# S4 convolution beside multi-query attention on Trainium2: the query projection in m-tiles of 128 rows, with heads that lie across two tiles

## The chip, the cores and the metric

The kernel runs on one core of one Trainium2 chip. The metric is the device time of one execution in microseconds; before the change its median is 1229.37 us over three runs. The core has five engines that matter here: TensorE (PE; its weight loads are listed apart as PEld), VectorE (DVE), ScalarE (ACT), GpSimd (POOL) and SyncE (SP). SP, ACT and POOL also issue DMAs, each in the order of its own instructions. TensorE writes only to PSUM, from where VectorE or ScalarE take the result.

## The reference: what is computed

Two independent parts, joined on the last axis. Part A convolves an input of 2048 steps and 576 channels with a kernel made from 128 complex modes per channel (an S4 layer). Part B is attention with 32 query heads of 18 columns that share one key and one value head:

```python
q = (x @ wq).reshape(B, S, 32, 18).transpose(0, 2, 1, 3)   # x: 1 x 2048 x 576
k = x @ wk
v = x @ wv
scores = einsum("bhqd,bkd->bhqk", q, k) * 18 ** -0.5
o = einsum("bhqk,bkd->bhqd", softmax(scores), v)
b = o.transpose(0, 2, 1, 3).reshape(B, S, 576) @ wo
```

Everything is float32.

## The kernel before

The program is one stream of instructions per engine, for TensorE, ScalarE and VectorE in an order that Python writes out while it builds the kernel.

**Attention** goes through four chunks of 512 queries. Within a chunk it goes through eight groups of four heads, and within a group through 16 blocks of 128 keys; two heads at a time form a pair. For each pair and key block, `scores` (L412, matmuls at L419) makes keys times queries in PSUM with a two-pass float32r product, 55 rows deep: 18 rows of the rounded query against the rounded key, 18 against the key's remainder, 18 of the query's remainder against the rounded key, and a row that holds a bound to be subtracted. `exponentials` (L427) applies exp on ScalarE, and `product` (L711, L718) multiplies with the values, four heads side by side in four column tiles of 32 of the array. Three pairs form one round of the main loop (L730); `step` counts key blocks of four heads, 512 in all.

**The query projection** fills gaps of this loop. `qproj` (L313) makes one m-tile, up to 126 of the 576 query rows (seven heads, the last m-tile has 72 rows and four heads, `MT` at L28) for the 512 queries of a chunk. It goes over two column halves of 256 and five k-slices of 128; each of these ten units is a `matmul4` (L164), which puts up to four column tiles of 32 rows into the array, one matmul each. In the trace each float32 matmul is two instructions. VectorE copies the result out of PSUM as `qh` (rounded), makes the remainder `ql` and the row maximum `ab` (L331 to L334). `qh` and `ql` have one buffer each. `queries` (L350) stores `qh` twice and `ql` once into the DRAM tensor `qd` of the chunk (L368, on POOL's queue; for chunk 0's first tile on SP's), so that each head finds its rows for the augmented product. Then it makes `aw`, the row maxima times the largest key of each row (`kmax`), sums them by head with a small matmul against the selector `sel` (`up`, L379), takes the maximum over heads on VectorE (`un`), and stores the negative as the bound's row (`sh`, L390 to L399). `fetch` (L402) brings a pair's rows back from `qd` into one of five `aug` buffers, on SP's queue, as soon as the whole pair has been stored and a buffer is free.

**The order of the fill work.** `fill` (L680) decides between rounds what else TensorE does: `prep` (normalizing), `side` (projections and output projection) and `conv` (part A). A planner's clock (class `Clock`, L61) carries estimated times; a unit of the query projection is charged 0.465. `late` (L633) compares the units done with a target at each quarter of the loop; the comparison at L694 holds `side` back when it is ahead of 0.64 units a step. Part A's sine batches on ScalarE wait until eight units of side work are due beside them, or 16 steps have passed (L1257 to L1261).

**The opening** (`setup`, L209). Inputs are loaded on the SP and ACT queues. TensorE projects the keys and chunk 0's first m-tile together, k-slice by k-slice (L268 to L270). `place(c)` (L278) puts the keys of chunk c into the augmented key tensor `kaug` with six DMAs on SP. The order on SP is: keys of chunk 0, of chunk 1, the stores of chunk 0's first m-tile, keys of chunks 2 and 3, then the weights of m-tiles 2, 3 and 4 (L295 to L300). Weights 0 and 1 are loaded earlier. The main loop starts with key chunk 0 and reaches chunk 2 at its ninth key block.

The program keeps a second, general attention behind a flag that is only taken when the bound is large (L784); with these inputs it does not run.

Of the kernel before, what the change touches and what calls it, by code (L numbers as in the profile page):

```python
# [17 lines left out]
P = 128  # L18
# [8 lines left out]
DT = KT[:4] + [(512, 64)]  # L27
MT = [(0, 126), (126, 126), (252, 126), (378, 126), (504, 72)]  # L28
# [143 lines left out]
class Attention:  # L172
# [33 lines left out]
    def load_wq(self, m):  # L206
        self.nc.sync.dma_start(self.wq[m], self.a["wq"][m, :, :, :MT[m][1]])

    def setup(self, tp, conv):  # L209
# [6 lines left out]
        self.wq = [cp.tile([P, 5, n], F32, name=f"wq{m}_sb") for m, (_, n) in enumerate(MT)]  # L216
        self.wo = cp.tile([P, 5, D], F32, name="wo_sb")
        self.sel = cp.tile([P, 8], F32, name="sel_sb")
        spread = tp.tile([P, 130], F32, name="spread_sb")
# [3 lines left out]
        self.kmax = cp.tile([P, 1], F32, name="kmax")  # L223
# [17 lines left out]
        nc.scalar.dma_start(self.wq[0], a["wq"][0, :, :, :MT[0][1]])  # L241
# [5 lines left out]
        nc.scalar.dma_start(self.sel, a["sel"][:, 0:8])  # L247
        nc.scalar.dma_start(spread, a["sel"][:, 8:138])
# [26 lines left out]
        V.tensor_scalar(km[:, 0:4], spread[:, 126:130], km[:, 4:5], None, op0=ALU.mult)  # L275
# [8 lines left out]
        nc.tensor.matmul(pk[:126, :], spread[:, 0:126], km[:, 0:4], start=True, stop=True)  # L284
# [5 lines left out]
        V.tensor_reduce(self.kmax[:126, :], pk[:126, :], axis=AX.X, op=ALU.max)  # L290
# [22 lines left out]
    def qproj(self, c, m, xt):  # L313

        nc, V, K = self.nc, self.V, self.k
        m0, mn = MT[m]
        self.q_left = 10
        yield "p", K.fill, False
        ps = self.bank(CT, f"q{c}_{m}")
        for f in range(2):  # L320
            sl = slice(f * 256, f * 256 + 256)
            for k in range(5):
                matmul4(nc, ps[:, sl], self.wq[m][:, k, :], xt[:, k, sl], start=(k == 0), stop=(k == 4))
                K.pe(0.465)
                self.q_left -= 1
                self.units += 1
                if (f, k) != (1, 4):
                    yield "p", 0.0, True
        K.v = max(K.v, K.t)
        qh, ql, ab = self.operands(c, m)  # L330
        V.tensor_copy(qh[:mn, :], ps[:mn, :])  # L331
        V.tensor_tensor(ql[:mn, :], ps[:mn, :], qh[:mn, :].bitcast(F32), op=ALU.subtract)
        K.filled()
        V.tensor_reduce(ab[:mn, 0:1], qh[:mn, :].bitcast(F32), axis=AX.X, op=ALU.max, apply_absolute_value=True)  # L334
        yield from self.queries(c, m, qh, ql, ab)

# [5 lines left out]
    def first_queries(self, ps):  # L342
        nc, V, mn = self.nc, self.V, MT[0][1]
        qh, ql, ab = self.operands(0, 0)
        nc.scalar.activation(qh[:mn, :], ps[:mn, :], AF.Copy)
        V.tensor_reduce(ab[:mn, 0:1], ps[:mn, :], axis=AX.X, op=ALU.max, apply_absolute_value=True)
        V.tensor_tensor(ql[:mn, :], ps[:mn, :], qh[:mn, :].bitcast(F32), op=ALU.subtract)
        yield from self.queries(0, 0, qh, ql, ab)

    def queries(self, c, m, qh, ql, ab):  # L350

        nc, V, K = self.nc, self.V, self.k
        m0, mn = MT[m]
        h0, h1 = m0 // DH, (m0 + mn) // DH
        if m == 0:
            self.qd[c] = self.dr.tile([H, 55, CT], F32, tag="qd", name=f"qd{c}")
        qd = self.qd[c]

        n0 = 4 if (c, m) == (0, 0) else 0
        for h in range(n0):  # L360
            t = self.aug[h // 2]
            for row, src in ((0, qh), (18, qh), (36, ql)):
                b = 64 * (h % 2) + row
                q = nc.scalar if h // 2 == 1 and row < 36 else nc.gpsimd
                q.dma_start(t[b:b + 18, :].bitcast(F32), src[h * DH:h * DH + DH, :].bitcast(F32))
        def store(q):
            for row, src in ((0, qh), (18, qh), (36, ql)):
                q.dma_start(qd[h0 + n0:h1, row:row + 18, :], src[n0 * DH:mn, :].bitcast(F32))  # L368
        if n0 == 0:
            store(nc.gpsimd)  # L370
        self.first = False
        yield "v", 0.0, False
        aw = self.p2.tile([P, P], F32, tag="aw", name=f"aw{c}_{m}", bufs=1)

        V.tensor_scalar(aw[:mn, :], ab[:mn, 0:1].broadcast_to([mn, P]), self.kmax[:mn, 0:1], 1.002, op0=ALU.mult, op1=ALU.mult)
        yield "p", max(K.v + 0.4, K.fill), False

        up = self.bank(8, f"up{c}_{m}")
        matmul4(nc, up, aw[:mn, :], self.sel[:mn, 0:8])  # L379
        K.pe(0.1)  # L380
        K.v = max(K.v, K.t + 0.3)
        un = self.p2.tile([P, 1], F32, tag="un", name=f"un{c}_{m}", bufs=4)
        V.tensor_reduce(un, up, axis=AX.X, op=ALU.max)
        K.filled()
        if self.ubound is not None:
            u2 = self.p2.tile([P, 1], F32, tag="u2", name=f"u2_{c}_{m}", bufs=4)
            V.tensor_tensor(u2, un, self.ubound, op=ALU.max)
            un = u2
        self.ubound = un
        sh = self.p2.tile([8, CT], F32R, tag="sh", name=f"sh{c}_{m}", bufs=1)  # L390
        V.tensor_scalar(sh, un[0:8, 0:1].broadcast_to([8, CT]), -1.0, None, op0=ALU.mult)
        for pr in range(n0 // 2):
            (nc.scalar, nc.sync)[pr].dma_start(self.aug[pr][54:119:64, :].bitcast(F32), sh[0:2, :].bitcast(F32))
# [5 lines left out]
        q.dma_start(qd[h0 + n0:h1, 54, :], sh[:h1 - h0 - n0, :].bitcast(F32))  # L399
        self.queried = c * H + h1  # L400
# [204 lines left out]
    def prepare(self):  # L605

        nc = self.nc
        while True:
            if not self.todo:
                yield "w", 0.0, False  # L610
                continue
            c, ms = self.todo[0]

            while ms[0] == 0 and (self.outs or c == NCH - 1 and self.due < 1 << 30):
                yield "w", 0.0, False
            self.todo.pop(0)
            self.busy = True
            if c == NCH - 1 and ms[0] == 0:
                self.part = self.xp.tile([P, 4, D], F32, tag="x", name="part")
                self.rest = {(t, n, m) for t in range(4) for n in range(2) for m in range(4)}  # L620
            if ms[0] == 3:
                self.w4 = self.p1.tile([P, D], F32, tag="ob", name="w4")
                self.b4 = self.p2.tile([P, P], F32, tag="aw", name="b4", bufs=1)
                nc.sync.dma_start(self.w4, self.a["wo4"])
                nc.sync.dma_start(self.b4, self.a["b4"])
            yield from self.normalize(c, ms)
            if c < NCH - 1:
                self.begin_output(self.outproj(c))
            elif ms[0] < 3:
                self.begin_output(self.outproj_part(c, ms, self.part))  # L630
            self.busy = False

    def late(self):  # L633

        s = self.step
        if self.due < 128 and self.due - s < 2 * self.q_left + 14:
            return True
        return (90, 180, 270, 302)[s // 128] - self.units > LEFT * (128 * (s // 128) + (120, 120, 120, 116)[s // 128] - s)
# [18 lines left out]
    def main(self, conv, flag):  # L657
# [22 lines left out]
        def fill(then):  # L680
# [3 lines left out]
            while more:  # L684
# [4 lines left out]
                for st in (prep, side, conv) if urgent else (prep, conv, side):  # L689
# [4 lines left out]
                    wait = then - K.t - (1.2 if st is side and not urgent and not side.holds and self.units > 0.64 * self.step + HEAD else 0.15)  # L694
# [89 lines left out]
def general_attention(tc, a, flag):  # L784
# [3 lines left out]
    with ExitStack() as ctx:  # L788
# [3 lines left out]
        wq = cp.tile([P, 5, 5, 126], F32, name="gwq")  # L792
# [12 lines left out]
        nc.sync.dma_start(wq, a["wq"].rearrange("m p k n -> p m k n"))  # L805
# [15 lines left out]
        with tc.For_i(0, 16, 1) as i:  # L821
# [4 lines left out]
            for h in range(H):  # L826
                ps = ps_t.tile([P, CT], F32, tag="t", name=f"gq{h}")
                for k, (k0, kn) in enumerate(KT):
                    nc.tensor.matmul(ps[:DH, :P], wq[:kn, h // 7, k, h % 7 * DH:(h % 7 + 1) * DH], xt[:kn, k, :], start=(k == 0), stop=(k == 4))
# [473 lines left out]
def layout(inputs):  # L1303
# [6 lines left out]
    wq = np.zeros((640, 630), np.float32)  # L1310
    wq[:D, :D] = g["B_wq"]
    a["wq"] = np.ascontiguousarray(wq.reshape(5, P, 5, 126).transpose(2, 1, 0, 3))
# [11 lines left out]
    sel = np.zeros((P, 138), np.float32)  # L1324
    i = np.arange(126)
    sel[i, i // DH] = 1.0
    for c in range(NCH):
        sel[32 * c + i % DH, 8 + i] = 1.0
        sel[32 * c:32 * c + 32, 134 + c] = 1.0
# [41 lines left out]
```

## Time and profile before

| | |
|---|---|
| runs | 1229.19, 1229.37, 1229.40 us |
| the profiled execution's own time | 1229.19 us |
| its span in the profile | 1226.8 us |
| TensorE clock granted, mean | 0.991 |
| HBM traffic | 55.64 MB read, 42.89 MB written |
| products with the values on TensorE (L718) | 518.0 us busy, 4096 instructions |
| scores on TensorE (L419) | 361.2 us busy, 2048 instructions |

The profile shows one execution, with times from the start of its span. A group's row reads: line, engine, operation, what it writes and reads with the shapes, how many; then busy microseconds, mean nanoseconds of one; then the idle time of the engine just before them and what ended it. Busy time of a group on TensorE is the union of instructions that overlap in the array, so the mean of one is no price. A row of the timeline reads: start, duration of the merged stretch, engine, line, operation, count, and in brackets the idle time before. The chain that ended last goes back from the end, at each step to what released it. A line can be a helper's: L99, L103, L107 and L111 are the recording wrappers around VectorE's operations, L169 is `matmul4`.

### The profile page before, as it was taken

The numbers are of one execution on the slowest core, as the hardware profiler recorded it, in microseconds if no ns is written. First come the engines' busy times: TensorE is split into PE (matmuls) and PEld (weight loads), VectorE is DVE, ScalarE is ACT, GpSimd is POOL, SyncE is SP. The second block draws the span as 40 slices with busy tenths as digits, with TensorE's granted clock in tenths as the row PEclk, the third lists the DMA queues.
The fourth block names the chain that finished last, engine by engine and source line by source line (L and its number), as shares of the span: only waits on it lengthen the run. The fifth ranks groups of instructions, "written<-read, shape, count | busy, mean of one in ns | idle before, by whom it ended". The sixth has DMA issues, their size and how long they took to land.

```text
span 1226.8 us, 32559 instructions
## 1 busy us (share of the span) xinstructions
PE 1145.4 (93%) x13762; PEld 471.2 (38%) x13762; DVE 991.1 (81%) x1604; ACT 1032.7 (84%) x1091; POOL 53.8 (4%) x93
## 2 busy tenths in 40 slices
PE   5799999999889999989999989999989999899997
PEld 1343334434333434434434433444333444334333
DVE  4667988987986995897895997796899897797753
ACT  2588998879978887898988998888989988999992
POOL 2010100000100000000000000000010000000000
PEclk9899999999999999999999999999999999999999
DMA  7542223122233112033123121312222312012111
GB/s 221 170 117 83 85 105 117 38 76 92 85 131 114 45 61 85 30 119 95 65 90 110 63 88 38 102 55 91 67 80 103 114 36 82 17 48 86 44 41 41
DMA packets 57947, 102.07 MB, mean 83 GB/s; under 512 B 14524, under 2 KB 25148, under 8 KB 57285
## 3 DMA queue, kind: packets, MB, share of 16 engines
q1 hardware_dynamic: 47029, 85.31, 21.0%
q0 software_dynamic: 10080, 14.05, 4.3%
q8 instruction: 110, 1.80, 0.6%
q10 hardware_dynamic: 688, 0.57, 0.2%
q14 instruction: 40, 0.33, 0.1%
HBM read 55.64 MB, written 42.89 MB: 80 GB/s over the span
## 4 chain that ended last, share of the span: by engine, by line
PE 62%; DVE 22%; ACT 7%; issue 5%; DMA 3%; SPq 1%; ACTq 0%; DVEq 0%
PE ops L718 25%; PE s L419 18%; ACT P L427 7%; DVE acc L99 4%; PE op L169 4%; DVE ks L99 3%; PE q L169 3%; PE kg L1081 3%; PE iy L169 3%; DVE tab L99 3%; DVE pt L99 2%; DMA xr<-xT 2%; PE hu L169 1%; PE lu L169 1%; PE hk L169 1%
## 5 line engine op out<-in xcount | busy, mean ns | idle before, releaser
L427 ACT ACTIVATE P<-s 128x1024 f32<-128x1024 f32 x1024 | 967.8, 1030 | 156.7 <-PE s L419 151.9
L718 PE MATMUL ops<-P,v_sb 128*32 128x512 f32 x4096 | 518.0, 599 | 7.3 <-DVE o L103 7.2
L419 PE MATMUL s<-aug,kaug 55*128 55x512 f32 x2048 | 361.2, 441 | 23.6 <-ACT P L427 19.9
L419 PEld LDWEIGHTS s<-aug,kaug 55*128 55x128 f32 x2048 | 168.8, 185 | 332.1 <-ACT P L427 298.0
L718 PEld LDWEIGHTS ops<-P,v_sb 128*32 128x32 f32 x4096 | 116.9, 110 | 151.4 <-issue 115.7
L169 PE MATMUL q<-x,wq_sb 128*32 128x256 f32 (+2 forms) x1480 | 105.4, 402 | 6.2 <-DMA wq_sb<-wq 4.6
L169 PE MATMUL op<-wo_sb,oT 126*32 126x288 f32 (+1 forms) x1088 | 78.3, 410 | 8.9 <-DVE ob L103 7.2
L169 PEld LDWEIGHTS q<-x,wq_sb 128*32 128x32 f32 (+1 forms) x1480 | 46.8, 111 | 61.6 <-issue 33.4
L103 DVE COPY ksb<-kg 128x192 f32<-128x192 f32 x48 | 17.4, 362 | 55.2 <-PE kg L1081 55.0
L99 DVE TENSOR_TENSOR tab<-tab,tt 128x576 f32<-128x576 f32 (+1 forms) x72 | 59.2, 822 | 1.8
L99 DVE TENSOR_TENSOR tab<-tab 128x576 f32<-128x576 f32 (+1 forms) x72 | 59.1, 822 | 1.7
L99 DVE TENSOR_TENSOR tt<-f,sum 128x576 f32<-128x576 f32 (+1 forms) x72 | 58.9, 818 | 0.0
L99 DVE TENSOR_TENSOR tab<-sum,r 128x576 f32<-128x576 f32 (+1 forms) x72 | 58.9, 818 | 0.0
L99 DVE TENSOR_TENSOR tab<-r,dif 128x576 f32<-128x576 f32 (+1 forms) x72 | 58.8, 817 | 0.0
L169 PEld LDWEIGHTS op<-wo_sb,oT 126*32 126x32 f32 (+1 forms) x1088 | 30.9, 109 | 50.2 <-issue 19.4
L99 DVE TENSOR_TENSOR acc<-acc,pt 128x1728 f32<-128x1728 f32 (+2 forms) x36 | 48.7, 1354 | 0.7
L99 DVE TENSOR_TENSOR pt<-us,ks 128x1728 f32<-128x1728 f32 (+2 forms) x36 | 48.7, 1352 | 0.4
L368 POOL DMA_DIRECT2D qd<-qh x38 | 24.0, 637 | 505.0 <-DVE qh L103 505.0
L169 PE MATMUL iy<-w,dft_sb 128*32 128x192 f32 x768 | 38.3, 335 | 7.6 <-DVE ql L99 7.4
L1081 PEld LDWEIGHTS kg<-tab 128*32 128x32 f32 x2304 | 35.8, 110 | 25.1 <-issue 7.3
L1081 PE MATMUL kg<-tab 128*32 128x64 f32 x2304 | 41.8, 220 | 1.8 <-DVE ql L99 1.2
L99 DVE TENSOR_TENSOR ks<-ks 128x576 f32<-128x576 f32 (+1 forms) x48 | 40.9, 853 | 0.7
(130 smaller groups left out, 916.1 us busy)
## 6 DMA issues: line engine op xcount, KB each, us to landing
aug<-qd SPq DMA_DIRECT2D x124, 110.0 KB
od<-o SPq DMA_DIRECT2D x31, 256.0 KB
qd<-qh POOLq DMA_DIRECT2D x30, 252.0 KB, 5.3
fr<-stage SPq DMA_DIRECT2D x10, 624.0 KB
u<-u SPq DMA_DIRECT2D x12, 384.0 KB
kd<-ksb SPq DMA_DIRECT2D x12, 384.0 KB
kt<-kd SPq DMA_DIRECT2D x48, 96.0 KB
outa<-u SPq DMA_DIRECT2D x12, 384.0 KB
```

The costliest lines, as they stand in the source:

```text
L99: return self.v.tensor_tensor(out, *a, **k)
L103: return self.v.tensor_copy(out, *a, **k)
L169: nc.tensor.matmul(ps[j:e], w[:, j:e], x, start=start, stop=stop, tile_position=(0, j))
L368: q.dma_start(qd[h0 + n0:h1, row:row + 18, :], src[n0 * DH:mn, :].bitcast(F32))
L419: nc.tensor.matmul(ps[:, j, :], self.kaug[r, kb * P:(kb + 1) * P], t[r, :], start=True, stop=True)
L427: nc.scalar.activation(pt, ps, AF.Exp, scale=SCALE)
L718: nc.tensor.matmul(o_ps[32 * j:32 * j + 32, :], self.v[:, kb, :], pts[2 * n + j // 2][:, j % 2, :], start=(kb == 0), stop=(kb == 15), tile ...
L1081: nc.tensor.matmul(ps[32 * g:32 * g + 32, d, :], t[:, :32], t[:, 32:], start=(j == 0), stop=(j == 1), tile_position=(0, 32 * g))
```

## The change

The m-tiles become 128, 128, 128, 128 and 64 rows, so that a head of 18 rows can begin in one tile and end in the next. Heads are counted to the tile in which they end (7, 14, 21, 28, 32, as before).

- `qproj`: the first four m-tiles keep two column halves of five k-slices, with four column tiles of 32 rows. The last one, 64 rows, takes both column halves at once: column tiles 0 and 1 hold its rows for queries 0 to 255, tiles 2 and 3 for queries 256 to 511. It has five units, and `qh`, `ql`, `ab` work on 256 columns.
- `pieces` and `store`: the rows of a tile go to `qd` in pieces, an end of a head, a run of whole heads, a beginning of a head; the last tile's in two column halves as well.
- `up`: for m-tiles 1 to 4 a second product adds the previous tile's share of the head that lies across (`self.aw` is the previous `aw`, which therefore has two buffers).
- `kmax` has a column for each m-tile; four of them come from new small products (`kmx4`) in the opening.
- `sh` is 256 columns wide and is read twice by its DMA.
- The opening's order on SP: weights of m-tile 2, keys of chunk 2, weights of 3, keys of chunk 3, weights of 4.
- The planner's targets follow the new number of units (80, 165, 250, 282 instead of 90, 180, 270, 302; 0.60 instead of 0.64 units a step). The general attention and the host's layout follow the new weights' shape.

```diff
+MQ = [(0, 128), (128, 128), (256, 128), (384, 128), (512, 64)]
+HQ = (0, 7, 14, 21, 28, 32)
...
         side.advance()
-        for c in range(2, NCH):
-            place(c)
 
         for m in range(2, 5):
             V.memset(self.wq[m][0:1, 0, 0:1], 0.0)
             self.load_wq(m)
+            if m < 4:
+                place(m)
         project(pv, 32, 4)
         V.tensor_copy(vt, pv)
+
+        pk = self.bank(16, "kmx4")
+        for m in range(1, 5):
+            for b, n in ((0, 128),) if m < 4 else ((0, 64), (64, 64)):
+                nc.tensor.matmul(pk[b:b + n, 4 * m - 4:4 * m], spread[:, 2 * m:2 * m + n], km[:, 0:4], start=True, stop=True, tile_position=(0, b))
+        V.tensor_reduce(self.kmax[:, 1:5], pk.rearrange("p (m c) -> p m c", c=4), axis=AX.X, op=ALU.max)
...
-        for f in range(2):
-            sl = slice(f * 256, f * 256 + 256)
+        for f in range(nf):
             for k in range(5):
-                matmul4(nc, ps[:, sl], self.wq[m][:, k, :], xt[:, k, sl], start=(k == 0), stop=(k == 4))
+                for j in range(4):
+
+                    o = slice(32 * j, 32 * j + 32)
+                    i = o if m < 4 else slice(32 * (j % 2), 32 * (j % 2) + 32)
+                    x = slice(256 * f, 256 * f + 256) if m < 4 else slice(256 * (j // 2), 256 * (j // 2) + 256)
+                    nc.tensor.matmul(ps[o, 256 * f:256 * f + 256], w[:, k, i], xt[:, k, x], start=(k == 0), stop=(k == 4), tile_position=(0, 32 * j))
...
+    @staticmethod
+    def pieces(m, h0):
+
+        m0, mn = MQ[m]
+        i = max(m0, h0 * DH)
+        while i < m0 + mn:
+            h, d = divmod(i, DH)
+            n = (m0 + mn - i) // DH if d == 0 else 0
+            rows = (n, 0, DH) if n else (1, d, min(DH - d, m0 + mn - i))
+            yield (i - m0, h) + rows
+            i += rows[0] * rows[2]
...
         def store(q):
             for row, src in ((0, qh), (18, qh), (36, ql)):
-                q.dma_start(qd[h0 + n0:h1, row:row + 18, :], src[n0 * DH:mn, :].bitcast(F32))
+                for i, h, n, d, nd in self.pieces(m, n0):
+                    for f in range(1 if m < 4 else 2):
+                        cs, i1 = (slice(0, CT), i) if m < 4 else (slice(256 * f, 256 * f + 256), i + 64 * f)
+                        q.dma_start(qd[h:h + n, row + d:row + d + nd, cs], src[i1:i1 + n * nd, :cs.stop - cs.start].bitcast(F32))
...
-        matmul4(nc, up, aw[:mn, :], self.sel[:mn, 0:8])
+        matmul4(nc, up, aw, self.sel[:, 8 * m:8 * m + 8], stop=(m == 0))
+        if m > 0:
+            n = 8 if m == 4 else 4
+            for b in range(0, n, 4):
+                matmul4(nc, up[:, b:b + 1], self.aw, self.sel[:, 39 + m:40 + m], start=False, stop=(b + 4 == n))
+        self.aw = aw
```

More of the change, by code (lines that the diff above doesn't have):

```diff
@@ L206, in load_wq @@
     def load_wq(self, m):
-        self.nc.sync.dma_start(self.wq[m], self.a["wq"][m, :, :, :MT[m][1]])
+        self.nc.sync.dma_start(self.wq[m], self.a["wq"][m, :, :, :MQ[m][1]])
     def setup(self, tp, conv):
         nc, cp, a, V = self.nc, self.cp, self.a, self.V
-        self.wq = [cp.tile([P, 5, n], F32, name=f"wq{m}_sb") for m, (_, n) in enumerate(MT)]
+        self.wq = [cp.tile([P, 5, n], F32, name=f"wq{m}_sb") for m, (_, n) in enumerate(MQ)]
         self.wo = cp.tile([P, 5, D], F32, name="wo_sb")
-        self.sel = cp.tile([P, 8], F32, name="sel_sb")
-        spread = tp.tile([P, 130], F32, name="spread_sb")
+        self.sel = cp.tile([P, 45], F32, name="sel_sb")
+        spread = tp.tile([P, 140], F32, name="spread_sb")
         self.kaug = cp.tile([P, S], F32R, name="kaug")
@@ L222, in setup @@
         self.v = cp.tile([P, 16, 32], F32, name="v_sb")
-        self.kmax = cp.tile([P, 1], F32, name="kmax")
+        self.kmax = cp.tile([P, 5], F32, name="kmax")
         wkv = tp.tile([P, 5, 64], F32, name="wkv_sb")
@@ L283, in setup @@
         pk = self.bank(4, "kmx")
-        nc.tensor.matmul(pk[:126, :], spread[:, 0:126], km[:, 0:4], start=True, stop=True)
+        nc.tensor.matmul(pk, spread[:, 0:128], km[:, 0:4], start=True, stop=True)
         for k in range(2, 4):
@@ L389, in queries @@
         self.ubound = un
[L390 to L391 removed]
+        sh = self.p2.tile([8, 256], F32R, tag="sh", name=f"sh{c}_{m}", bufs=1)
+        V.tensor_scalar(sh, un[0:8, 0:1].broadcast_to([8, 256]), -1.0, None, op0=ALU.mult)
+        two = lambda t, n: t[:n, :].bitcast(F32).unsqueeze(1).broadcast_to([n, 2, 256])
         for pr in range(n0 // 2):
[L393 removed]
+            (nc.scalar, nc.sync)[pr].dma_start(self.aug[pr][54:119:64, :].bitcast(F32).rearrange("p (a n) -> p a n", a=2), two(sh, 2))
             self.ready.add(pr)
@@ L693, in fill @@
                     spare = credit - 0.3 if st is not side or urgent or late or side.holds else 0.0
-                    wait = then - K.t - (1.2 if st is side and not urgent and not side.holds and self.units > 0.64 * self.step + HEAD else 0.15)
+                    wait = then - K.t - (1.2 if st is side and not urgent and not side.holds and self.units > 0.6 * self.step + HEAD else 0.15)
                     if st.go(self.step, max(spare, wait, 0.3 * (st is side and side.holds and conv.lags(self.step) and credit > -1.0)), holder()):
@@ L804, in load @@
                 nc.sync.dma_start(t[:64, 4, :], src[512:, :])
-        nc.sync.dma_start(wq, a["wq"].rearrange("m p k n -> p m k n"))
+        for m in range(5):
+            nc.sync.dma_start(wq[:, :, m * P:m * P + P], a["wq"][m])
         load(wo, a["wo"])
@@ L828, in general_attention @@
                 for k, (k0, kn) in enumerate(KT):
-                    nc.tensor.matmul(ps[:DH, :P], wq[:kn, h // 7, k, h % 7 * DH:(h % 7 + 1) * DH], xt[:kn, k, :], start=(k == 0), stop=(k == 4))
+                    nc.tensor.matmul(ps[:DH, :P], wq[:kn, k, h * DH:(h + 1) * DH], xt[:kn, k, :], start=(k == 0), stop=(k == 4))
                 V.tensor_copy(qt[:, h, :], ps[:DH, :P])
@@ L1323, in layout @@
     a["ident"] = np.eye(P, dtype=np.float32)
-    sel = np.zeros((P, 138), np.float32)
-    i = np.arange(126)
-    sel[i, i // DH] = 1.0
+    sel = np.zeros((P, 185), np.float32)
+    for m, (m0, mn) in enumerate(MQ):
+        for i in range(P):
+            d = m0 + i % mn
+            sel[i, 8 * m + d // DH - HQ[m] + i // mn * 4] = 1.0
+        if m > 0:
+            i = np.arange(HQ[m] * DH - m0 + P, P)
+            sel[i, 39 + m] = 1.0
+    i = np.arange(136)
     for c in range(NCH):
-        sel[32 * c + i % DH, 8 + i] = 1.0
-        sel[32 * c:32 * c + 32, 134 + c] = 1.0
+        sel[32 * c + i % DH, 45 + i] = 1.0
+        sel[32 * c:32 * c + 32, 181 + c] = 1.0
     a["sel"] = sel
```

54 lines of the change are left out of this document (28 added, 26 removed).

## The prediction

> **What bounds the kernel now.** I read the page first: busy shares, the chain that ended last, the costliest group.
>
> ```profile
> PE 1145.4 (93%) x13762; PEld 471.2 (38%) x13762; DVE 991.1 (81%) x1604; ACT 1032.7 (84%) x1091; POOL 53.8 (4%) x93
> ...
> PE 62%; DVE 22%; ACT 7%; issue 5%; DMA 3%; SPq 1%; ACTq 0%; DVEq 0%
> ...
> L427 ACT ACTIVATE P<-s 128x1024 f32<-128x1024 f32 x1024 | 967.8, 1030 | 156.7 <-PE s L419 151.9
> ```
>
> ScalarE's exponentials wait 151.9 us for scores, so TensorE sets the pace over most of the span. But the chain is VectorE for 22%: there are stretches where TensorE has slack, and a microsecond taken from TensorE is not worth a microsecond everywhere. I use these chain shares as weights: 0.62 for TensorE work spread over the span, 0.22 for VectorE work. They are an average over stages, which is the weakest step below.
>
> The second view is the chain in order of time, with the SP queue's timeline and the windows around it, for the opening.
>
> ```profile
> 37.34 5.86 DMA qd<-ql
> ...
> 49.36 3.18 DMA wq_sb<-wq
> 52.67 3.21 PE q L169 x32
> ```
>
> ```profile
> 35.83 1.46 SPq L368 DMA_DIRECT2D qd<-qh  x2
> 37.34 0.66 SPq L368 DMA_DIRECT2D qd<-ql  x1
> 38.04 0.55 SPq L399 DMA_DIRECT2D qd<-sh  x1
> 38.64 10.61 SPq L281 DMA_DIRECT2D kaug<-keys  x12
> 49.36 1.61 SPq L207 DMA_DIRECT2D wq_sb<-wq  x3
> ```
>
> ```profile
> 48.00:52.70 4.70, 0.13 (x6) 0.06 (x5) 4.63 (x6) 2.59 (x3) 0.54 (x1) 0.91 0.73 222
> 52.70:56.70 4.00, 4.00 (x42) 1.77 (x42) 3.18 (x5) 0.00 (x0) 0.00 (x0) 0.67 1.02 369
> ```
>
> The weights of the third m-tile stand behind twelve key placements on SP. They are issued at 49.36 and land 3.18 later; TensorE does nothing from 48.1 to 52.67, and the granted clock of the next 4 us is 0.67.
>
> **The projection units.** A unit is one k-slice over 256 columns. The groups by line, with the forms kept apart, show what the last m-tile costs now.
>
> ```profile
> L169 PE MATMUL q<-x,wq_sb 128*32 128x256 f32 x1060 | 97.3, 394 | 6.2 <-DMA wq_sb<-wq 4.6 <-DVE un L111 1.5
> L169 PE MATMUL q<-x,wq_sb 128*30 128x256 f32 x300 | 77.1, 396 | 0.0
> ...
> L169 PE MATMUL q<-x,wq_sb 128*8 128x256 f32 x80 | 19.3, 379 | 0.0
> ```
>
> ```profile
> 142.74 3.66 PE L169 MATMUL q<-x,wq_sb 128*32 128x256 f32 x64
> ```
>
> ```profile
> 907.03 3.65 PE L169 MATMUL q<-x,wq_sb 128*32 128x256 f32 x48
> ```
>
> Each matmul of the source is two instructions, so the 80 eight-column ones are 40 units: ten for each of four chunks. The run of 64 at 142.74 is eight units of a full m-tile, eight instructions each; the run of 48 at 907.03 is eight units of the last m-tile, six each. Both take about 3.65 us: the column tiles run side by side, and three cost what four cost, 0.456 us a unit. With its two column halves side by side the last m-tile has five units instead of ten: 20 units fewer, 9.1 us of TensorE, and 80 instructions. Widening the others from 126 to 128 rows only fills the fourth tile from 30 to 32 columns: nothing.
>
> **The split heads' bound.** A head that lies across two m-tiles adds a second product to `up`: eight one-column instructions for m = 1 to 3, sixteen for m = 4, so 160 in all, 20 sets as large as a present `up`.
>
> ```profile
> 119.78 0.18 PE up L169 x8
> ```
>
> ```profile
> 45.21 0.25 PE L169 MATMUL up<-sel_sb,aw 126*32 126x8 f32 x8
> ...
> 45.30 1.90 PE L718 MATMUL ops<-P,v_sb 128*32 128x512 f32 x16
> ```
>
> On the chain such a set takes 0.18; at 45.21 the next matmul follows 0.09 behind its start. Between these, 0.14 a set: 2.8 us (1.8 to 3.6). TensorE nets 9.1 - 2.8 = 6.3 us, times 0.62: **3.9 us saved**. Per-chunk thresholds and the 0.60 pacing only follow the smaller unit count; I price them at nothing. `aw` has two buffers, so keeping the previous one alive adds no wait.
>
> **VectorE.**
>
> ```profile
> L103 DVE CAST qh<-q 72x512 fp32r<-72x512 f32 x4 | 2.7, 680 | 0.0
> ...
> L107 DVE TENSOR_SCALAR sh<-u 8x512 fp32r<-8x512 f32 x19 | 7.9, 415 | 0.7
> ...
> L107 DVE TENSOR_SCALAR aw<-ab,kmax 126x128 f32<-126x128 f32 x16 | 4.7, 293 | 0.6
> ...
> L552 DVE TENSOR_TENSOR o_last<-o_last,bc 128x256 f32<-128x256 f32 x2 | 0.8, 422 | 2.2 <-PE bc L572 1.2 <-PE bc L566 1.0
> ```
>
> The last m-tile's copy, subtraction and maximum go from 512 to 256 columns: 680 to about 422 ns, three operations, four chunks: 3.1 us. `sh` at 256 columns lies between 293 (128) and 415 (512), about 334: 19 times 0.08 is 1.5 us. Together 4.6 us, times 0.22: **1.0 us saved**.
>
> **The stores.** A tile's rows now begin and end inside heads: two pieces for m = 0, three for m = 1 to 3, two in two halves for m = 4. Each goes out three times, so POOL issues 174 stores instead of 57.
>
> ```profile
> L368 POOL DMA_DIRECT2D qd<-qh x38 | 24.0, 637 | 505.0 <-DVE qh L103 505.0
> ...
> L368 POOL DMA_DIRECT2D qd<-ql x19 | 11.7, 614 | 1.8 <-issue 1.5 <-DVE ql L99 0.3
> ```
>
> ```profile
> qd<-ql POOLq DMA_DIRECT2D x15, 252.0 KB, 6.6
> ```
>
> ```profile
> 900.54 1.25 POOL L368 DMA_DIRECT2D qd<-qh  x2 [9.75 <-DVE qh L103]
> 905.56 0.55 POOL L399 DMA_DIRECT2D qd<-sh  x1 [3.17 <-DVE sh L107]
> ...
> 913.35 1.31 POOL L368 DMA_DIRECT2D qd<-qh  x2 [7.25 <-DVE qh L103]
> ...
> 317.56 1.31 POOL L368 DMA_DIRECT2D qd<-qh  x2 [9.88 <-DVE qh L103]
> ...
> 334.34 1.26 POOL L368 DMA_DIRECT2D qd<-qh  x2 [10.04 <-DVE qh L103]
> ```
>
> That is 117 times 0.62, 73 us more on a queue busy for 53.8. Who waits? First `sh`, queued behind the stores: POOL waited 3.17 for it at 905.56, six more stores take 3.7, so it can leave half a microsecond late. Second `qh` and `ql`, which have one buffer: VectorE may not write the next tile until the stores have landed, and conv's work and the evacuations of PSUM queue behind it. The shortest gap is 900.54 to 913.35. Nine stores at 0.62 and a landing of 6.6 take 12.2 us, and the last m-tile now comes some 1.4 us sooner there: about a microsecond of waiting, once or twice. I take **1.0 us lost** (0 to 2).
>
> The Trainium skill speaks against this edit: "DMA: Bandwidth & Descriptors" (section Anatomy of one DMA, SWDGE path) gives each such transfer a fixed 2.0 us, and its rules for kernel authors ask for small transfers to be merged. Taken one after another at that price, nine stores would be about 20 us instead of 12.2. The 637 ns at which two stores follow each other here speak for overlapping, and I keep 12.2; the other result is a rival below.
>
> **The opening.** SP's stores of chunk 0's first tile become six: 35.83 to 38.00 for three is 0.72 each, so 2.2 us more. Ahead of the placements of key chunk 2 then stands one weight load (1.61/3 = 0.54), ahead of chunk 3 two; the third follows. So the weights go out at 38.64 + 2.2 = 40.8 and land at 44.0, well before 48.1. Chunk 2's six placements at 0.88 end at 46.7 and land about 3 us later; its first block serves the sixth group of three scores, which stands behind the weights' units, at 52 or later. Chunk 3's end at 52.6, for a group three groups on, nine exponentials or 8.5 us later (967.8/1024 each). What follows on SP shifts by 2.2 us:
>
> ```profile
> 59.64 15.03 SPq L408 DMA_DIRECT2D aug<-qd  x10
> ...
> 72.67 0.73 PE L419 MATMUL s<-aug,kaug 55*128 55x512 f32 x4
> ```
>
> The first fetched pair, issued at 61.9, serves the scores that are now at 72.67, then about 69: covered by several microseconds.
>
> Not covered: `ql` of m = 1 waited for the SP store (37.34 + 5.86 = 43.2). That store now comes 2.2 us later, so `ql`, `ab`, `aw` are late by as much, and TensorE waits that long at `up` (45.21). It then reaches the third m-tile's units at 48.1 + 2.2 = 50.3 instead of 52.67: 2.4 us. And without the long hole the 32 instructions take half of 3.65 instead of 3.21: 1.4 us. **3.8 us saved** (0 to 6.0: nothing if another load is late in its place, 4.6 + 1.4 if `ql` is not delayed).
>
> The new `kmx4` products:
>
> ```profile
> 26.60 0.38 PE L284 MATMUL kmx<-km,spread_sb 128*126 128x4 f32 x2
> ...
> 32.97 1.32 PE L419 MATMUL s<-aug,kaug 55*128 55x512 f32 x6 [1.73 <-DMA aug<-sh]
> ```
>
> Two take 0.38, ten about 1.9, under a wait of 1.73 for a DMA they do not touch: nothing, or 0.3 if the cover fails. The selector load grows by 37 columns on 128 partitions, 19 KB: nothing.
>
> **The sum.** The profiled execution took 1229.19 us (span 1226.8 and 2.4 around it), the lowest of the three runs, 0.2 below their median. 1229.2 - 3.8 - 3.9 - 1.0 + 1.0 = **1221.5 us**.
>
> **Rivals.** (1) *TensorE is the path everywhere.* Then the loop gives 6.3 to 7.3 instead of 3.9, and the opening up to 6.0: 1216. For it: ScalarE's 151.9 us of waiting. Against it: the run of 48 at 907.03 lay beside ScalarE's sine work and ended in a wait:
>
> ```profile
> 906.57 1.28 ACT L1000 ACT_TABLE_LOAD   x1
> ...
> 913.93 1.51 PE L169 MATMUL iy<-w,dft_sb 128*32 128x192 f32 x32 [3.25 <-DVE ql L99]
> ```
>
> There fewer units buy nothing. (2) *The opening's gain does not come*: another load or the longer store chain holds TensorE as long, so the early weights don't do what they are moved for. 1221.5 + 3.8 = 1225. (3) *Slower: the sine batches lose their cover.* Conv holds a batch until eight units are due beside it, or 16 steps have passed (L1257 to L1261). The last m-tile has five, so it never counts; a batch that met it now waits, or runs with nothing beside it, and TensorE loses the 3.65 us that lay under the batch at 906.57. One or two batches eat half of the gain; from three on it is gone: 1221.5 + 3 x 3.65 = 1232. Against it: a full m-tile follows the last one in each chunk but the fourth, as the run of 64 at 142.74 does, and a held batch can wait for that. (4) *Stores one after another.* At about 20 us for nine and 27 for twelve, the gap of 12.8 above overruns by 8, the one of 16.8 from chunk 1's last tile (317.56) to chunk 2's first (334.34) by 10. VectorE stands still for 18 us, and TensorE's evacuations with it: about 1240. Its rule is the page's named above.
>
> **Chances.** The forecast 0.42, TensorE everywhere 0.13, no gain in the opening 0.23, sine batches 0.16, serial stores 0.06. 0.2% is 2.5 us, about what a measurement of this kernel can tell from no change: faster means below 1226.9. The forecast, rival 1 and half of rival 2 are faster: 0.67. The other half of rival 2 and two lost batches (0.05) are the same: 0.16. Rival 3 from three batches and rival 4: 0.17. The range runs from 1214, rival 1 at its best (1229.2 - 6.0 - 7.3 - 1.0, stores at nothing: 1214.9, rounded down), to 1230, which takes in rival 2 and two lost batches (1228.8).
>
> **What would show it.** Right: 13762 - 80 + 160 + 10 = 13852 TensorE instructions; `q` in 1400 with no 30- or 8-column form; 320 `up`; no wait of `q` for wq_sb; POOL near 126 us; a chain that still waits for qd<-ql, about 2 us later, then runs on TensorE. Wrong: a wait of scores for kaug or aug near 50 or 70 us; `qh` or `ql` waiting for qd in several tiles; exponentials missing around the sine batches for longer than now; or equal ScalarE waiting although `q` shrank.

## The result, and the profile after

The changed kernel takes 1220.97 us (median of 6 runs, 1218.61 to 1223.97), the kernel before on the same chip 1229.49 (6 runs, 1229.19 to 1230.74): a ratio of 0.9922, 95% interval 0.9905 to 0.9939. The forecast was 1221.5. The profiled execution took 1222.7 us. Three rows of its page, and two from the list of TensorE's groups (line, operation, tiles, count, then busy time and mean, then the idle time before them):

```profile
span 1220.9 us, 32948 instructions
...
PE 1142.6 (94%) x13852; PEld 468.1 (38%) x13852; DVE 983.8 (81%) x1608; ACT 1032.8 (85%) x1091; POOL 119.5 (10%) x210
...
L467 ACT ACTIVATE P<-s 128x1024 f32<-128x1024 f32 x1024 | 967.9, 1029 | 152.9 <-PE s L459 150.9
```

```profile
L338 PE MATMUL q<-x,wq_sb 128*32 128x256 f32 x1360 | 85.2, 383 | 1.0 <-DVE un L116 1.0
...
L174 PE MATMUL up<-sel_sb,aw 128*32 128x8 f32 (+1 forms) x320 | 6.3, 180 | 16.5 <-DVE aw L112 15.9 <-DVE scu L104 0.4
```

The counts are those of the forecast: 13852 instructions on TensorE, 1360 + 40 of the projection, 320 `up`; POOL is busy 119.5 us (forecast 126). But TensorE is busy only 2.8 us less than before, and ScalarE waits for scores 150.9 us, hardly less than before's 151.9. Less work on TensorE has not become less waiting for TensorE, which the prediction had named as a sign of being wrong. And `up` waits 15.9 us for `aw` (2.1 before).

The opening, in the chain in order of time (start, microseconds, what), then SP's own queue, then TensorE's timeline:

```profile
37.60 4.96 DMA qd<-ql
...
44.75 0.39 PE up L174 x16
45.15 3.46 PE ops L758 x16
48.61 1.58 PE s L459 x6
50.18 1.86 PE q L338 x32
```

```profile
34.36 2.46 SPq L402 DMA_DIRECT2D qd<-qh  x4
36.88 1.19 SPq L402 DMA_DIRECT2D qd<-ql  x2
38.11 0.29 SPq L439 DMA_DIRECT2D qd<-sh  x1
38.50 1.12 SPq L212 DMA_DIRECT2D wq_sb<-wq  x1
39.66 4.55 SPq L286 DMA_DIRECT2D kaug<-keys  x6
44.31 0.76 SPq L212 DMA_DIRECT2D wq_sb<-wq  x1
```

```profile
44.75 0.39 PE L174 MATMUL up<-sel_sb,aw 128*32 128x8 f32 x16 [3.55 <-DVE aw L112]
44.99 3.62 PE L758 MATMUL ops<-P,v_sb 128*32 128x512 f32 x16
...
50.11 1.93 PE L338 MATMUL q<-x,wq_sb 128*32 128x256 f32 x32
...
68.91 1.34 PE L459 MATMUL s<-aug,kaug 55*128 55x512 f32 x6
```

The weights go out at 38.50 instead of 49.36, and `q` no longer waits for them. The third m-tile's 32 instructions start at 50.11 (52.67 before, forecast 50.3) and take 1.93 instead of 3.21. The scores that stood at 72.67 stand at 68.91: 3.8 us sooner, the forecast's number. (Not all of it comes from the moved weights: in this execution the first exponential already starts at 31.38 instead of 33.84.) What stands in place of the hole is `up`'s wait of 3.55 for the store chain, and after it sixteen matmuls in 3.62 instead of 1.90.

Later in the loop the batches of sines look different from before. TensorE and ScalarE around the first batch of the changed kernel:

```profile
132.95 1.28 ACT L1041 ACT_TABLE_LOAD   x1
...
133.42 2.80 PE L338 MATMUL q<-x,wq_sb 128*32 128x256 f32 x48
...
141.27 0.29 PE L174 MATMUL up<-sel_sb,aw 128*32 128x8 f32 x8 [5.05 <-DVE aw L112]
141.37 3.65 PE L758 MATMUL ops<-P,v_sb 128*32 128x512 f32 x16
```

Before, 80 instructions of the projection stood at the first batch, whose table load starts at 145.32: the 64 of the row at 142.74, and 16 more at 148.10. Now it is 48, six units, then a wait of 5.05 and sixteen matmuls at half speed. To see what such places cost I compared the start of each of the 1024 exponentials, counted from 0, with its start in the profile before (us, negative is sooner; from the trace's rows of ScalarE; the kernels of the second and third column are told below):

| exponential | changed | changed, second chip | ten planned units |
|---|---|---|---|
| 32 | -3.8 | -3.1 | -5.5 |
| 64 | -3.8 | -0.7 | -4.4 |
| 96 | +0.9 | +3.4 | -4.4 |
| 256 | -1.4 | +2.5 | -4.6 |
| 448 | -12.5 | -9.8 | -10.2 |
| 512 | -8.3 | -5.6 | -10.3 |
| 1023 | -5.4 | -5.7 | -6.2 |

The opening's gain is lost again at the first batch (4.7 us between numbers 64 and 96). Between 256 and 448 the changed kernel's profile wins 11.0 us, but not all of that is less work: 4.2 are gone again at 512 (49 `kg` instructions now stand behind number 448 instead of ahead of it, and TensorE idles 4.6 us more there), and 3.4 are two stretches of half clock that the kernel before has in this part, at 335 and 489, and the changed kernel has not. At the end all three stand alike.

### The profile page after: what moved, and what is told of

Same layout as the page of the kernel before. It is cut to its first block, busy times and chain, and to the rows that moved or that the text cites. A ratio compares the mean times of both kernels' runs of the same rounds, so it can differ in the third digit from the quotient of the medians.

```text
span 1220.9 us, 32948 instructions
## 1 busy us (share of the span) xinstructions
PE 1142.6 (94%) x13852; PEld 468.1 (38%) x13852; DVE 983.8 (81%) x1608; ACT 1032.8 (85%) x1091; POOL 119.5 (10%) x210
## 4 chain that ended last, share of the span: by engine, by line
PE 63%; DVE 22%; ACT 6%; issue 4%; DMA 3%; SPq 1%; POOL 0%; DVEq 0%; ACTq 0%
PE ops L758 26%; PE s L459 18%; ACT P L467 6%; PE op L174 4%; DVE acc L104 3%; DVE tab L104 3%; PE q L338 3%; DVE ks L104 3%; PE kg L1122 3%; PE iy L174 3%; DVE pt L104 2%; DMA xr<-xT 1%; PE hu L174 1%; PE hk L174 1%; DMA qd<-ql 1%
## 5 line engine op out<-in xcount | busy, mean ns | idle before, releaser
L467 ACT ACTIVATE P<-s 128x1024 f32<-128x1024 f32 x1024 | 967.9, 1029 | 152.9 <-PE s L459 150.9
L402 POOL DMA_DIRECT2D qd<-qh x116 | 67.6, 588 | 533.5 <-DVE qh L108 533.4
L338 PE MATMUL q<-x,wq_sb 128*32 128x256 f32 x1360 | 85.2, 383 | 1.0 <-DVE un L116 1.0
L338 PEld LDWEIGHTS q<-x,wq_sb 128*32 128x32 f32 x1360 | 40.5, 110 | 46.7 <-issue 21.0
L104 DVE TENSOR_TENSOR u<-u,iy 128x384 f32<-128x384 f32 x24 | 13.3, 554 | 31.1 <-PE iy L174 30.8
```

The lines of the kernel that those rows point to most:

```text
L104: return self.v.tensor_tensor(out, *a, **k)
L338: nc.tensor.matmul(ps[o, 256 * f:256 * f + 256], w[:, k, i], xt[:, k, x], start=(k == 0), stop=(k == 4), tile_position=(0, 32 * j))
L402: q.dma_start(qd[h:h + n, row + d:row + d + nd, cs], src[i1:i1 + n * nd, :cs.stop - cs.start].bitcast(F32))
L467: nc.scalar.activation(pt, ps, AF.Exp, scale=SCALE)
```

## The experiments

Every kernel was timed in five rounds against the kernel before on its chip (before's medians there: 1232.17, 1231.43 and 1230.88 us). A ratio is to these.

**The order of weights and keys alone**, in the kernel before:

```diff
-        for c in range(2, NCH):
-            place(c)
         for m in range(2, 5):
             self.load_wq(m)
+            if m < 4:
+                place(m)
```

> The kernel before with one part of the change alone: on SP's queue the weights of m-tiles 2, 3 and 4 come between the keys' chunks 2 and 3. TensorE, VectorE and ScalarE keep their order. My theory: the hole of 4.6 us at 48.1 closes and the 1.4 us of half clock behind it go; the query remainder's wait stays as it is (43.2), since the stores are still three: 4 to 6 us faster, 1223.5 to 1225.5. Rival, that something else is late in the weights' place (the keys of chunk 2): within 1.5 us of before, with scores waiting for kaug.

Measured: 1233.14 us, ratio 0.9998 (0.9982 to 1.0014). Nothing that could be measured: the interval leaves a gain of 2.2 us at most, where 4 to 6 were expected. Its chain and TensorE's timeline:

```profile
55.69 8.49 DMA u<-u
...
64.20 8.35 DMA aug<-qd
...
72.60 0.50 PE s L419
```

```profile
49.40 1.93 PE L169 MATMUL q<-x,wq_sb 128*32 128x256 f32 x32
...
72.01 1.08 PE L419 MATMUL s<-aug,kaug 55*128 55x512 f32 x2 [3.15 <-DMA aug<-qd]
73.02 3.42 PE L718 MATMUL ops<-P,v_sb 128*32 128x512 f32 x16
```

The wait for the weights is gone here too, and the third m-tile starts 3.3 us sooner than before (49.40). But the rows fetched behind the inputs `u` come late: 3.15 us of waiting, and then sixteen matmuls in 3.42 instead of 1.92. That is rival 2, the second late load, in this profile of the kernel before.

**The old order in the changed kernel:**

```diff
+        for c in range(2, NCH):
+            place(c)
         for m in range(2, 5):
             self.load_wq(m)
-            if m < 4:
-                place(m)
```

> The changed kernel with the weights of m-tiles 2 to 4 again behind all keys on SP's queue. The other engines' orders are those of the changed kernel. If the opening's part of the gain is 3.8 us as forecast: 1224 to 1226, with q waiting some 6 us for wq_sb. If the early weights only moved the hole to the wait at up, as the profile after suggests for its own execution: 1222 to 1223.5.

Measured: 1228.34 us, ratio 0.9962 (0.9946 to 0.9978). Against the changed kernel's 0.9922 and, measured again below, 0.9936, the order is worth 0.26% to 0.40% there, 3.2 to 4.9 us; each of these ratios is uncertain by 2 to 3 us. In its waits the old one is back:

```profile
PE q L338 <- DMA wq_sb<-wq: 3.6, 1, 3.6
```

So the same edit is worth some 4 us in one kernel and nothing that could be measured in the other. In the first profile of the changed kernel SP comes to the fetches at 60.02 and no score waits for them in the opening; with the edit alone it comes to them at 62.58, and one does. Most of these 2.6 us are there already when the first tile's stores start (34.36 against 36.80), ahead of anything that the edit moves. In the second profile of the changed kernel SP comes to them at 60.94, and the same late fetch is there, but small:

```profile
PE s L459 <- DMA aug<-qd: 0.9, 2, 0.7
```

So when the fetches come differs from execution to execution, and why the edit alone gains nothing is shown by one profile only.

**The units back, unplanned**: each of the last m-tile's five slots issues two units, the first five of the ten into the unused half of the bank; the planner counts five.

```diff
-                for j in range(4):
+                todo = [(f, k)] if m < 4 else [(1 - u // 5, u % 5) for u in (2 * k, 2 * k + 1)]
+                for (g, kk), j in ((t, j) for t in todo for j in range(4)):
```

> The changed kernel with the last m-tile's five units done twice: each of its five slots issues two units, the first five of the ten into the unused half of the bank. The planner is told nothing, so the orders stay; 20 units of TensorE (9.1 us) come back, nothing else. With the chain's weight of 0.62: 5.6 us slower than the changed kernel, 1226.5. Rival, TensorE everywhere: 9 us, 1230. Rival, the last m-tile lies where VectorE or ScalarE sets the pace: under 2 us.

Measured: 1228.13 us, ratio 0.9965 (0.9950 to 0.9979): 3.6 to 5.3 us slower than the changed kernel. Taken alone this says that units are worth what I had put on them. The next two, and the table at the end of this section, speak against it.

**Fewer units in the kernel before**: of the last m-tile's second column half only the last k-slice is computed.

```diff
-                matmul4(nc, ps[:, sl], self.wq[m][:, k, :], xt[:, k, sl], start=(k == 0), stop=(k == 4))
+                matmul4(...) if m < 4 or f == 0 else k == 4 and matmul4(nc, ps[:, sl], self.wq[m][:, k, :], xt[:, k, sl])
```

> The kernel before without four of the five k-slices of the last m-tile's second column half: 16 units fewer (7.3 us of TensorE), in the order of before; the queries of heads 28 to 31 are then made from part of the sum in half of the columns. With the weight of 0.62: 4.5 us faster than before. If fewer units are worth more in the changed kernel only because its order is another: under 2 us. TensorE everywhere: 7 us.

Measured: 1233.34 us, ratio 1.0011 (0.9995 to 1.0027). Sixteen units fewer, and no gain: the interval leaves 0.6 us at most, where 4.5 were expected. One of TensorE's waits in its profile, and the same wait before:

```profile
PE iy L169 <- DVE ql L99: 10.8, 3, 5.4
```

```profile
PE iy L169 <- DVE ql L99: 7.4, 3, 3.3
```

Part of the time that the units leave is spent waiting for the same step of VectorE that comes behind them.

**Ten planned units in the changed kernel**: two column halves for the last m-tile (the first into the unused half), with the planner's numbers of before (90, 180, 270, 302 and 0.64). VectorE's work stays at 256 columns.

```diff
-        w, nf = self.wq[m], 2 if m < 4 else 1
+        w, nf = self.wq[m], 2
...
-        n = 256 * nf
+        n = 512 if m < 4 else 256
```

> The changed kernel with ten planned units for the last m-tile again: its five k-slices over both halves run twice, first into the unused half of the bank, each as a unit of its own for the planner, whose targets are those of before (90, 180, 270, 302; 0.64). Stores, bounds, weights' order and 256 columns on VectorE stay. If the loop's gain is the 20 units, wherever they lie: 4 to 6 us slower than the changed kernel, 1226 to 1228. If it is the order that the planner finds with fewer units to place: 6 us or more slower, 1228 to 1231, or as slow as the old order happens to be. Rival, neither: within 2 us.

Measured: 1222.45 us, ratio 0.9930 (0.9913 to 0.9947), the same as the changed kernel with its five; 4 to 6 us of difference, which were expected of the units, would have shown. Its page:

```profile
PE 1147.8 (94%) x14012; PEld 475.4 (39%) x14012; DVE 986.2 (81%) x1605; ACT 1032.9 (85%) x1091; POOL 118.3 (10%) x210
...
L339 PE MATMUL q<-x,wq_sb 128*32 128x256 f32 x1520 | 95.2, 387 | 2.0 <-DVE un L116 1.9
```

TensorE is busy 5.2 us more than in the changed kernel and, with spans of 1220.8 and 1220.9, idle 5.3 us less. The rows of waits show where the changed kernel's idle time lies; first the changed kernel, then this one:

```profile
PE up L174 <- DVE aw L112: 15.9, 5, 5.0
...
PE ops L758 <- DVE o L108: 9.5, 13, 1.6
PE op L174 <- DVE ob L108: 5.3, 4, 2.3
```

```profile
PE iy L174 <- DVE ql L104: 11.2, 4, 3.9
...
PE op L174 <- DVE ob L108: 3.8, 2, 2.2
PE ops L759 <- DVE o L108: 3.8, 4, 1.7
PE up L174 <- DVE aw L112: 2.5, 2, 1.4
```

The wait for VectorE's query step changes its name, from `iy` to `up`, and stays: 13.7 us here, 15.9 there. The waits for VectorE to empty the accumulators of a round (`o`, `ob`) fall from 14.8 to 7.6. So most of what the shorter last m-tile takes from TensorE, TensorE spends idle, above all waiting for VectorE; the rest is in the table at the end of this section.

This run also bears on the order. Written as a sequence of output tiles with repeats merged, TensorE's order in its trace agrees with the kernel before in 96%, the changed kernel's in 42%. It has nearly the old order, and has the whole gain.

**The stores cut alone**, in the kernel before, into as many pieces as the change has (at the ends of whole heads):

```diff
+                cuts = [0, n - 1, n] if m == 0 else [0, 1, n - 1, n] if m < 4 else [0, 1, n]
```

> The kernel before with its stores cut into as many pieces as the changed kernel has (2, 3, 3, 3 and 4 for the five m-tiles, three times each), at heads' borders; 174 stores on POOL instead of 57, six on SP in the opening. My theory: the wait of the remainder in the opening grows by 2.2 us, little else: 1 to 3 us slower than before, 1230.5 to 1232.5. Rival, stores that follow one another at 2 us or more: 15 us or more slower, with VectorE waiting for qd in most tiles.

Measured: 1231.23 us, ratio 0.9993 (0.9977 to 1.0009). Nothing that could be measured; the interval excludes a cost of more than 1.1 us. In this kernel the last m-tile still comes 12.8 us after the one ahead of it in the last chunk, and no `ql` of the loop waits for a store.

**The second product for `up` alone**, with a selector column of zeros, in the kernel before:

```diff
+        if m > 0:
+            n = 8 if m == 4 else 4
+            for b in range(0, n, 4):
+                matmul4(nc, up[:, b:b + 1], aw[:mn, :], self.sel[:mn, 7:8], start=False, stop=(b + 4 == n))
```

> The kernel before with 160 more instructions of up, as many as the changed kernel has: second products with a selector column of zeros, so that the values stay. Orders otherwise those of before. Forecast: 2.8 us of TensorE times 0.62, 1.7 us slower. Rival, each set stands on the path with more than its 0.14 us: 3.6 us or more. Rival, hidden: under 1 us.

Measured: 1229.58 us, ratio 0.9993 (0.9978 to 1.0009). Nothing that could be measured; the interval excludes a cost of more than 1.1 us, and 1.7 were expected.

**The changed kernel again**, on the second chip:

> The changed kernel once more, for a second profile and for times on this chip. If its spread of 5 us comes from stretches of half clock: the profile has another number of them than the first, and the steps between the two profiles' exponentials are some 1.7 us each and stand at those places; 0.992 of before. If it comes from loads: the steps stand in the opening.

Measured: 1222.83 us, ratio 0.9936 (0.9913 to 0.9959). Both expectations hold in part. TensorE runs at half clock for 23.9 us of the loop in this profile and for 27.3 in the first, and steps between the two stand where these stretches differ: 2.4 us between exponentials 32 and 64, where only this one has a stretch (at 72.6), and 1.1 and 1.2 between 640, 768 and 896, where only the first has them (at 906.9 and 1046.8). But the first exponential also comes 1.5 us later here, with a wait of 1.5 us for the input `xr` that is 0.4 in the first profile.

**The first tile's stores on POOL**, in the changed kernel, so that `ql` no longer waits for SP:

```diff
-        q = nc.gpsimd if n0 == 0 else nc.sync
+        q = nc.gpsimd
```

> The changed kernel with one queue changed: the stores of chunk 0's first m-tile and its bound go out on POOL, which is idle then, instead of SP, where they stand behind the keys of chunk 1. All orders on TensorE, VectorE and ScalarE stay. If the opening's gain was cut down by the wait of up for the query remainder (3.6 us, and half clock behind it in the profile after): 3 to 6 us faster than the changed kernel, 1215 to 1218, with no such wait. Rival, another load sets the pace there anyway: within 1 us of it, 1220 to 1222.

Measured: 1221.69 us, ratio 0.9919 (0.9898 to 0.9939). TensorE's timeline:

```profile
46.37 0.31 PE L174 MATMUL up<-sel_sb,aw 128*32 128x8 f32 x16
46.52 1.90 PE L758 MATMUL ops<-P,v_sb 128*32 128x512 f32 x16
...
68.03 1.37 PE L459 MATMUL s<-aug,kaug 55*128 55x512 f32 x6
```

`up`'s wait and the half speed behind it are gone, and yet the scores at 68.91 come only 0.9 us sooner. (The first exponential of this execution starts 2.4 us later, at 33.76 against 31.38; from there on the stretch is 3.3 us shorter.) In the time nothing is left of it that could be measured; the intervals of this run and of the changed kernel leave room for part of the 3 to 6 us that were expected.

**The planner's numbers alone**, each set in the other kernel. The new ones in the kernel before:

```diff
-        return (90, 180, 270, 302)[s // 128] - self.units > ...
+        return (80, 165, 250, 282)[s // 128] - self.units > ...
...
-  self.units > 0.64 * self.step + HEAD
+  self.units > 0.6 * self.step + HEAD
```

> The kernel before with the changed kernel's planner numbers alone (80, 165, 250, 282; 0.60). Nothing else changes, only the order. Forecast: nothing, within 2 us of before. If the order by itself is worth several microseconds either way, it shows here: 3 us or more up or down, with new idle time of TensorE at the sine batches or without.

Measured: 1254.68 us, ratio 1.0191 (1.0170 to 1.0213), 23 us slower. The opposite edit in the changed kernel:

> The changed kernel with the planner numbers of before (90, 180, 270, 302; 0.64), which ask for more units than there are. Forecast: nothing, within 2 us of the changed kernel. If the order is worth several microseconds: 3 us or more either way.

Measured: 1244.99 us, ratio 1.0118 (1.0100 to 1.0135), 22 to 24 us slower than the changed kernel. Both were expected within 2 us. The last exponential of the kernel before with new numbers, and of the kernel before:

```profile
1217.99 1.02 ACT L427 ACTIVATE P<-s 128x1024 f32<-128x1024 f32 x1 [0.57 <-PE s L419]
```

```profile
1204.56 1.02 ACT L427 ACTIVATE P<-s 128x1024 f32<-128x1024 f32 x1 [0.57 <-PE s L419]
```

With spans of 1257.1 and 1226.8 there are 39 us behind the first and 22 behind the second: 17 of the 30 us between these two profiles are work left over for the end. The changed kernel with old numbers loses its time inside the loop: its last exponential comes 20 us later than the changed kernel's.

**A batch held until ten units are due**, in the changed kernel with the first stores on POOL:

```diff
-                if self.beside() >= 8 or step > st.asked + 16 or self.n < 0:
+                if self.beside() >= 10 or step > st.asked + 16 or self.n < 0:
```

> The changed kernel with the first stores on POOL and with sine batches that wait for ten units beside them instead of eight. In the profiles of the changed kernel TensorE idles 4.8 and 4.6 us in the first two batches of the loop (1.6 and 1.7 before). If that is lost cover: the two fall to about 2 and the time by some 4 us, 1216 to 1218. Rival: the idle time comes from VectorE's lateness, whatever lies beside; then within 2 us of the changed kernel, 1220 to 1222.

Measured: 1222.58 us, ratio 0.9929 (0.9913 to 0.9946). The batches stand at the same exponentials as without the edit, and between the exponentials around the first one TensorE is idle for 4.8 us, by the trace's rows, as without it (1.6 in the kernel before). So the count was not what released them, and the rival's cure was not tried by this.

None of these is clearly faster than the changed kernel.

**What the profiles add up to.** At a granted clock of 0.50, half of TensorE's busy time is lost. With this loss taken out of the busy time, a span falls into three parts (us, from the traces' rows and clock records; one profile each):

| kernel | span | TensorE's work at full clock | idle | lost to half clock |
|---|---|---|---|---|
| before | 1226.8 | 1135.6 | 81.4 | 9.8 |
| before, fewer units | 1231.0 | 1130.0 | 87.2 | 13.8 |
| before, new planner numbers | 1257.1 | 1136.8 | 92.4 | 27.9 |
| changed | 1220.9 | 1131.3 | 78.3 | 11.3 |
| changed, second chip | 1220.5 | 1130.7 | 78.3 | 11.5 |
| ten planned units | 1220.8 | 1138.2 | 73.0 | 9.6 |
| units back, unplanned | 1226.7 | 1138.4 | 73.0 | 15.3 |
| changed, old planner numbers | 1241.4 | 1127.9 | 90.4 | 23.1 |

Fewer units do make TensorE's work less, by 5.6 us in the kernel before and by 6.9 between ten planned units and five, but idle time and half clock grow by as much or more (5.8 and 4.0; 5.3 and 1.7). And the two kernels with ten units have the same work and the same idle time: what the unplanned units cost against the planned ones, 5.9 us, is half clock. How much of it a kernel meets differs from run to run, but this difference stands in the other runs too: the mean clock lies between 0.985 and 0.989 in all nine runs with unplanned units, and at 0.991 or 0.992 in four of the six with planned ones.

## Why the prediction was right, and where not

The total was right to 0.5 us; its largest term was not, and the others are smaller than what could be measured.

**The opening, 3.8 us: right in size, in the profile partly by luck.** 3.8 in the profile at the scores of 68.91, 3.2 to 4.9 by undoing it. But 2.5 of the 3.8 in the profile are there at the first exponential, where the forecast has nothing; from the first to the 25th exponential the changed kernel takes 32.4 us in its first profile and 29.6 in its second, the kernel before 33.8. The step about the store chain was wrong inside: `ql` was to come 2.2 us late. SP started its stores 1.5 us sooner and the last one landed in 4.96 instead of 5.86, so `ql` came at 43.09, no later than before. The wait for `aw` was longer than forecast all the same (3.55 to 2.2), since TensorE got there sooner and VectorE's copy `qh` stood too, for 3.50 us; in the second profile the row of that wait, 4.03 us, names the stores of `qh`, which has one buffer. And rival 2 was no small case: it is what the profile shows when the new order stands alone in the kernel before.

**The projection units, 3.9 us with the `up` products taken off (5.6 for the units alone): wrong, about nothing.** The size of a unit was right: between ten and five units the group `q` goes from 95.2 to 85.2 us, for 9.1. The step that failed is the weight of 0.62, the chain's share of TensorE over the whole span. The units were not spread over the span; they stood in the last m-tile of each chunk, and there TensorE has waits for VectorE beside them that fill most of what they leave; more half clock takes the rest (fewer units before: 1.0011; ten planned units in the changed kernel: 0.9930). The 3.6 to 5.3 us of the unplanned units do not speak for the weight: against the changed kernel they add 7.1 us of work by the table, idle time gives 5.3 of these back, and 4.0 of what is left to pay are half clock.

**The planner's numbers, "nothing": right for numbers that fit, but without a reason.** They belong to the unit count. Ten units with the old numbers and five with the new are equal, so fitting numbers cost nothing that shows. But the wrong set costs 22 us or more, several times all other terms, and the forecast had no rival for that.

**The stores, 1.0 us, and the `up` products, 2.8 times 0.62: nothing that could be measured alone.** POOL's timeline in the changed kernel, at the place of the shortest gap, and the wait that I had looked for:

```profile
902.92 4.63 POOL L402 DMA_DIRECT2D qd<-qh  x8 [4.41 <-DVE qh L108]
907.53 2.55 POOL L402 DMA_DIRECT2D qd<-ql  x4
910.22 0.59 POOL L439 DMA_DIRECT2D qd<-sh  x1
```

```profile
DVE ql L104 <- DMA qd<-ql: 3.5, 2, 2.4
```

Twelve stores leave in 7.2 us, 0.6 each. VectorE's `ql` did wait twice, 1.09 of the 3.5 us in the opening and 2.36 at 904.99, the very place where the forecast had looked for it. The stores alone gave 0.9993, but there the last m-tile came too late to meet them, so what this one wait costs is not shown. The Trainium skill's 2.0 us for each ("DMA: Bandwidth & Descriptors", Anatomy of one DMA) is not a rate here; twelve at that price would be 24. Rival 4 is out.

**VectorE, 1.0 us: not measured alone.** It is busy 7.3 us less (983.8 for 991.1), where I had counted 4.6.

**Rival 3, the sine batches: it happened, and did not decide.** The first batch lost 4.7 us by the table (4.1 on the second chip), where 3.65 was forecast as the price; but the time comes back later, and ten planned units, which keep the batches' cover (1.6 us of idle at the first), end at the same time.

**What stays open.** With the old order the change is still worth 0.38% (0.22% to 0.54%), 4.7 us. Units, stores and `up`, each tried alone, give none of it. A new order of the fill work is not needed for it either, since ten planned units have the gain with nearly the old order. What is left is VectorE's shorter work, which no run tried alone, and what the parts do together. That the total came out right is in part luck: this rest took the place of the 3.9 us of the units.

## What to carry to other kernels

Do not weight a saving by an engine's share of the whole chain: find the places where the removed instructions stand and read what ends the next wait there; if it is another engine's step, the saving turns into a longer wait, and a longer wait can cost half clock on top. A transfer moved ahead of others is only worth what the next late transfer leaves, so try the move in each version of the kernel that it may go into. When fill work is placed by a planner with hand-set targets, the targets are part of the change and can cost more than all the rest.

## What the runs showed of the hardware

The granted clock of TensorE falls to 0.50 in stretches. The windows (microseconds, then each engine's busy time, the clock, the DMA share, GB/s) behind the two waits of the changed kernel, and, before, behind a wait of 3.25 us:

```profile
44.70:49.90 5.20, 5.15 (x38) 1.64 (x38) 5.06 (x9) 0.46 (x1) 3.28 (x6) 0.50 0.73 195
141.30:144.70 3.40, 3.40 (x24) 0.94 (x28) 3.33 (x10) 1.94 (x3) 2.52 (x5) 0.50 0.60 144
```

```profile
913.93:917.90 3.97, 3.97 (x64) 2.08 (x64) 3.83 (x6) 2.92 (x4) 1.36 (x3) 1.00 0.45 91
```

The waits of 3.55 and 5.05 us were followed by a clock of 0.50, the one of 3.25 was not. In the run with the stores cut alone the same wait is 3.25 us again, at 913.77, and a stretch of 0.50 follows, so the length of a wait alone does not decide. In the loop of the changed kernel such stretches last 3.4 us or twice that, and 3.4 us at 0.50 are 1.7 us of TensorE's work. The Trainium skill ("TensorE: Matmul & The Clock Gate", Part 1) gives a window of about 3.4 us and half the rate after an idle one. The trace agrees with the length and the half rate, but not with the idle window: ahead of five of the six stretches in the loop of the changed kernel's first profile TensorE had been busy for 0.8 to 1.5 of the last 3.4 us.

I had not expected what this does to the times. Over the six runs of the changed kernel the mean clock goes with the time: 0.990 and 0.991 in the three of 1218.61 to 1219.23 us, 0.986 to 0.989 in the three of 1222.7 to 1223.97. The same program differs by 5 us from run to run, more than any single term of the forecast.
